# Layer norms from residual rows kept in SBUF, their root on VectorE, and a moved piece of schedule, in a fused attention and feed-forward block

## The chip, the cores and the metric

The kernel runs on one core of one Trainium2 chip. The metric is the device time of one execution in microseconds. The shown runs of the kernel before took 876.0, 876.1 and 879.46 us, so the median is 876.1 us.

## What is computed

One transformer block over 2048 rows of width 512, with a modulation computed from a vector c. The attention has 32 heads of width 16 and works on four segments of 512 rows, with a causal softmax inside a segment and a memory that is carried from one segment to the next. The reference, cut to what matters:

```python
mod = silu(c) @ w_mod                     # six vectors sa, ca, ga, sb, cb, gb
h = layernorm(x) * (1 + ca) + sa
x = x + ga * attention(h)                 # per head: softmax part and memory part, then @ wo
h = layernorm(x) * (1 + cb) + sb
x = x + gb * (((h @ w_gate) * (h @ w_up)) @ w_down)
...
def layernorm(x):  return (x - mean(x)) / sqrt(var(x) + 1e-5)
```

## The kernel before

All products keep float32 accuracy by splitting both factors into a high and a low part and adding three products (names that end in H and L). A segment is four tiles of 128 rows by 512 columns, numbered t = 0 to 3.

**The attention loop** (L1122) has one iteration for each unit v of four heads of a segment, and five slots in an iteration. In a slot TensorE computes scores q (`q_step`, L270), which VectorE reduces to a maximum nm (L291); scores k (`k_step`, L311), which ScalarE exponentiates to pt (L329) and GpSimd masks (selection, L332); and once per iteration the product tb of pt with the values (`av_step`, L336). Between them `fill` (L1053) hands out the rest of the work in pieces from two generators, `fill_a` (L960) and, behind it, `fill_b` (L1023): the next segment's projections, the modulation, the memory, and at the end the output product and the norm ahead of the feed-forward part. A piece counts against a credit, so the written order of the pieces decides which work stands between which scores. `weave(a, b, at)` (L677) puts pieces of b behind chosen pieces of a. In the loop VectorE's instructions are chained in written order (`Chain`, L32, set at L1119); `pin` (L80) keeps an instruction behind the last TensorE instruction in the order of the program without a wait.

**The norms.** `ln_rows` (L167) takes the statistics of four tiles on VectorE (L174, L177), then the root: ScalarE's logarithm and exponential (L181, L183) give y, and one Newton step refines it. That step is five small instructions on 128x4 numbers, L187 to L191, on GpSimd for all norms but segment 0's first, which has them on VectorE. Then VectorE scales the four tiles in place (L194). Norms named a (tiles x) come ahead of attention, norms named c ahead of the feed-forward part. `ln_col` (L202) transposes the scaled tiles on TensorE (ctp), and ScalarE writes chf, the high part chH and GpSimd the low part chL (L222, L223).

**The output product.** `wo_load` (L467) loads a segment's attention rows (orl), `wo_op` (L475) splits them on ScalarE (oH, L497) and VectorE (L480). `wo_mm` (L537) makes one output row tile after the other: four groups of products into wops, then `wo_add` (L533) adds the residual tile xr, which was loaded from x by `xr_load` (L517), and stores the result to x1d in DRAM. For segments 0 and 1 `lnC` (L544) loads the four tiles back from x1d into tiles x (L548) and norms them. Segments 2 and 3 are normed later, in the feed-forward part (L1362 to L1367).

**Order at the end of attention.** `fill_a` ends with the first two output tiles of segment 0 (L1000), since the buffers of its pool are closed ahead of `fill_b` (`open_b`, L955). `fill_b` then makes the last two of segment 0, with the split of segment 1 woven in, all of segment 1 with segment 0's norm, the rest of that norm with segment 2's split, and segment 2 with segment 1's norm and the preparation of the first feed-forward weights (`prep`, L426: loads w, combinations L448, splits AH on ScalarE and AL).

**Modulation.** `mod_acc` (L624) scales four tiles wm on ScalarE (L626) and adds them on GpSimd (L628); `a_mod` (L917) then sums over partitions on TensorE (mc, gbps). Its four pieces for odd outputs are woven into projections K and Q of group 1 (L987 to L989).

Of the kernel before, what the change touches and what calls it, by code (L numbers as in the profile page):

```python
# [18 lines left out]
P = 128  # L19
# [39 lines left out]
def tile_kernel(ctx, tc, x, wq, wk_, wv, wo, beta, w_gate, w_up, w_down, c, w_mod, out):  # L59
# [107 lines left out]
    def ln_rows(pool, xt, s, pfx):  # L167
# [23 lines left out]
        eng.tensor_mul(y, y, b)  # L191
        yield 0.0
# [14 lines left out]
    def ln(pool, hpool, xt, s, sc, sh, pfx, hb, fast, kept_h=None):  # L207
# [5 lines left out]
        for d in range(KT):  # L213
# [15 lines left out]
            if pfx == "c" and d % 2 == 1:  # L229
                yield False  # L230
# [286 lines left out]
    def xr_load(s, pb, ts=range(4), tag="xr"):  # L517
        xrs = []
        for t in ts:
            xr = pb.tile([P, D], F32, tag=tag, name=f"xr{s}_{t}", bufs=2 if pb is wpool else 4)  # L520
            pin(nc.sync.dma_start(xr, x[rows(s, t), :]))
            xrs.append(xr)
        return xrs
# [13 lines left out]
    def wo_mm(s, us, xrs, ts=range(4)):  # L537

        for t, xr in zip(ts, xrs):
            ps = bank(f"wops{s}_{t}")  # L540
            yield from wo_row(ps, t, us, range(NG))
            wo_add(s, t, xr, ps)

    def lnC(s, pool, hpool, xpool, tag, nb):  # L544
        xt = []
        for t in range(4):
            a = xpool.tile([P, D], F32, tag=tag, name=f"x1_{s}_{t}", bufs=nb)
            nc.sync.dma_start(a, x1d[s][t])  # L548
            xt.append(a)
        yield 0.1  # L550
# [4 lines left out]
        for d in (0, 2, 1, 3):  # L555
# [3 lines left out]
            if d > 1:  # L559
                yield False  # L560
# [116 lines left out]
    def weave(a, b, at):  # L677

        i = 0
        for w in a:  # L680
            yield w
            if w:
                for _ in range(at.count(i)):
                    w = next(b, None)
                    if w or w is False:
                        yield w
# [245 lines left out]
    us = [[], [], []]  # L932

# [26 lines left out]
    def fill_a():  # L960
# [5 lines left out]
        for s in range(NSEG):  # L966
# [4 lines left out]
            for g in range(2 if s == 0 else 0, NG):  # L971
# [15 lines left out]
                if g == 1 and 0 < s < 3:  # L987
                    acc = mod_acc(r)
                    K, Q = weave(K, acc, (0, 2)), weave(Q, acc, (0, 2))  # L989
                if s == NSEG - 1 and g == 1:  # L990
                    xr0 = xr_load(0, wpool, (0, 1), "wor")
# [3 lines left out]
                if s == NSEG - 1 and g == NG - 1:  # L995
                    yield from weave(Q, ready, (0, 1, 2, 3))
# [3 lines left out]
                    yield from wo_mm(0, us[0], xr0, (0, 1))  # L1000
# [18 lines left out]
        while memq or memt:  # L1019
            yield mem_step() or 0.0  # L1020
            yield False
# [100 lines left out]
    for v in range(-2, NQ + 1):  # L1122
        rate[0] = 5.8 if v < 20 else 5.2
        on, prev = 0 <= v < NQ, 0 <= v - 1 < NQ
        for slot in range(5):
# [10 lines left out]
            if v == NQ and slot == 0:  # L1136
                assert B["orl_free"]
                o3 = wo_load(3, B["pb"])
                xr3 = xr_load(3, B["pb"])
            if v == NQ and slot == 2:  # L1140
# [379 lines left out]
```

## Time and profile before

| What | Value |
|---|---|
| Median of the shown runs | 876.1 us |
| The profiled execution's own time | 873.19 us |
| Its span | 871.1 us |
| Instructions | 14342 |
| Granted TensorE clock over the span | 0.995 |
| Moved by DMA | 139.45 MB, mean 160 GB/s |

The rows of this trace are of one execution. "L40" is the helper that chains instructions on an engine, so VectorE's rows in the loop are told apart by their tiles. In a row of the timeline come start, duration, engine, line, operation, output and inputs, form and count; a bracket at its end is the idle time of that engine before the row, and what ended it. A row that stands for several instructions of one kind has their count behind x. "PE" is TensorE, "DVE" VectorE, "ACT" ScalarE, "POOL" GpSimd and "SP" the queue that issues most transfers.

### The profile page before, as it was taken

Reading aid. Unit: us, or ns where it says so; the run is one execution under the profiler, and the core shown is the slowest. Engines: PE = TensorE matmul, PEld = TensorE weight load, DVE = VectorE, ACT = ScalarE, POOL = GpSimd, SP = SyncE. Lnnn points to the kernel's source line nnn. Section 1 sums busy time; section 2 is a strip of 40 time slices with the busy share of each in tenths; the row PEclk is TensorE's granted clock in tenths of the full one; section 3 lists DMA queues with packets and bytes.
Section 4 is the critical chain, followed back from the end, with each engine's and each line's share of the span. In section 5 each row is a group of like instructions: output and inputs, shape, how many; then the busy total and the mean of one; then the engine's idle time right before and its main releaser. Section 6 shows DMA issues by size and latency. Waiting matters only on the chain.

```text
span 871.1 us, 14342 instructions
## 1 busy us (share of the span) xinstructions
PE 828.9 (95%) x4823; PEld 581.2 (67%) x4824; DVE 658.9 (76%) x1728; ACT 474.5 (54%) x740; POOL 423.3 (49%) x564
## 2 busy tenths in 40 slices
PE   8989998989999899999988899999999999999998
PEld 5756565656565566655654577888778888887886
DVE  8688776988779877789888769888685966767532
ACT  3758757687676876678544664433354423333321
POOL 4536536565455764487323835998101755650000
PEclk9999999999999999999999999999999999999999
DMA  7773755567647565776794552654305232112032
GB/s 242 227 233 120 226 149 168 187 209 232 194 147 250 188 205 168 250 235 215 235 310 134 170 173 97 181 159 135 109 30 163 77 115 55 50 55 94 0 119 97
DMA packets 111355, 139.45 MB, mean 160 GB/s; under 512 B 18800, under 2 KB 70000, under 8 KB 111280
## 3 DMA queue, kind: packets, MB, share of 16 engines
q1 hardware_dynamic: 106016, 130.91, 48.7%
q10 hardware_dynamic: 5264, 7.62, 2.4%
q8 instruction: 38, 0.62, 0.3%
q14 instruction: 37, 0.30, 0.1%
HBM read 87.48 MB, written 50.76 MB: 159 GB/s over the span
## 4 chain that ended last, share of the span: by engine, by line
PE 66%; DVE 13%; ACT 7%; DMA 5%; POOL 3%; issue 3%; SPq 0%; ACTq 0%; POOLq 0%; DVEq 0%
PE g L90 23%; PE acc L90 14%; PE tb L90 5%; PE k L90 5%; PE q L90 5%; DVE q L40 4%; PE vps L90 4%; PE kps L90 2%; ACT pt L329 2%; PE wops L90 2%; PE qps L90 2%; DVE x L40 2%; DMA x1d<-xr 1%; DMA x<-in_x_dram 1%; PE mz L90 1%
## 5 line engine op out<-in xcount | busy, mean ns | idle before, releaser
L40 DVE CUSTOM_DVE_ANT_0 q<-q,cmask 128x384 f32<-128x384 f32 (+3 forms) x512 | 246.6, 508 | 57.7 <-PE q L90 47.8
L329 ACT ACTIVATE pt<-k 128x1024 f32<-128x1024 f32 x160 | 163.9, 1024 | 74.2 <-PE k L90 57.3
L332 POOL TENSOR_SCALAR_AFFINE_SELECT pt<-pt 128x256 f32<-128x256 f32 (+1 forms) x224 | 105.2, 484 | 154.9 <-ACT pt L329 149.8
L90 PE MATMUL q<-kst,qst 96*128 96x384 bf16 (+3 forms) x512 | 101.6, 300 | 12.1 <-DVE nm L40 11.5
L90 PE MATMUL k<-qst,kst 98*128 98x384 bf16 (+3 forms) x512 | 97.5, 303 | 9.4 <-ACT pt L329 9.1
L448 POOL TENSOR_TENSOR w<-w 128x256 f32<-128x256 f32 (+1 forms) x84 | 73.9, 893 | 56.0 <-DVE t L1205 37.9
L443 POOL TENSOR_TENSOR AL<-w,AH 128x512 fp32r<-128x512 f32 (+1 forms) x42 | 56.4, 1345 | 48.4 <-ACT AH L439 48.3
L90 PE MATMUL tb<-pt,v 128*32 128x512 f32 (+3 forms) x1024 | 77.4, 443 | 1.4 <-POOL pt L332 1.4
L90 PEld LDWEIGHTS <-kst 98*128 98x128 bf16 x512 | 38.5, 99 | 54.3 <-issue 48.0
L40 DVE DVE_READ_ACCUMULATOR2_ANT nm<- 128x1 f32 x512 | 72.3, 141 | 0.0
L90 PEld LDWEIGHTS <-qst 96*128 96x128 bf16 x512 | 43.4, 98 | 39.9 <-issue 15.9
L439 ACT ACTIVATE AH<-w 128x512 fp32r<-128x512 f32 (+3 forms) x88 | 47.2, 565 | 40.0 <-POOL w L448 26.7
L1462 DVE TENSOR_TENSOR mL<-mid,mH 128x512 fp32r<-128x512 f32 (+1 forms) x44 | 32.8, 750 | 41.5 <-ACT mH L1461 41.5
L90 PE MATMUL acc<-DH,mL 128*128 128x512 f32 x144 | 56.6, 393 | 0.9 <-DVE mL L1462 0.9
L90 PE MATMUL acc<-DH,mH 128*128 128x512 f32 x144 | 57.2, 397 | 0.0
L90 PEld LDWEIGHTS tb<-pt,v 128*32 128x32 f32 x1024 | 29.2, 111 | 41.1 <-issue 36.1
L90 PE MATMUL acc<-DL,mH 128*128 128x512 f32 x144 | 56.6, 393 | 0.0
L1461 ACT ACTIVATE mH<-mid 128x512 fp32r<-128x512 f32 (+1 forms) x44 | 27.1, 627 | 52.7 <-PE acc L90 51.5
L1254 ACT ACTIVATE p<-g 128x512 f32<-128x512 f32 (+1 forms) x22 | 13.1, 597 | 75.9 <-PE g L90 75.8
L443 DVE TENSOR_TENSOR AL<-w,AH 128x512 fp32r<-128x512 f32 (+3 forms) x44 | 35.2, 803 | 9.2 <-ACT AH L439 9.0
L358 ACT ACTIVATE tsb<-tb 128x512 f32<-128x512 f32 x32 | 19.1, 598 | 34.0 <-PE tb L90 34.0
L90 PE MATMUL g<-chH,AH 128*128 128x512 f32 (+1 forms) x88 | 34.8, 396 | 0.7 <-ACT p L1254 0.7
(286 smaller groups left out, 2064.3 us busy)
## 6 DMA issues: line engine op xcount, KB each, us to landing
kst<-kd SPq DMA_DIRECT2D x32, 384.0 KB
qst<-qd SPq DMA_DIRECT2D x32, 384.0 KB
td<-tsb ACTq DMA_DIRECT2D x28, 256.0 KB
wm<-in_w_mod_dram SPq DMA_DIRECT2D x24, 256.0 KB
kd<-k SPq DMA_DIRECT2D x16, 384.0 KB
qd<-q SPq DMA_DIRECT2D x16, 384.0 KB
w<-in_w_gate_dram SPq DMA_DIRECT2D x20, 256.0 KB
w<-in_w_up_dram SPq DMA_DIRECT2D x40, 128.0 KB
```

The source lines that it names most:

```text
L40: i = getattr(self.eng, name)(*a, **k)
L90: return pe(nc.tensor.matmul(*a, **k))
L329: lpt[0] = act.activation(pt, kp, AF.Exp, scale=0.25)
L332: sels[u, i] = nc.gpsimd.affine_select(w, w, pattern=[[0, w.shape[1]], [1, P]], compare_op=ALU.is_ge, fill=0.0, base=0, channel_multiplier=-1)
L358: act.activation(tsbs[u], tbs.pop(u), AF.Copy)
L439: i = act.activation(hi[sl], w[sl], AF.Copy)
L443: i = eng.tensor_sub(lo[sl], w[sl], hi[sl].bitcast(F32))
L448: i = ce.tensor_tensor(w[:, o, :, 0:n], w[:, x, :, 0:n], w[:, y, :, 0:n], op=op)
L1254: lcp[0] = act.activation(r["p1"], ps, AF.Copy)
L1461: pin(act.activation(mH[0:n], md[0:n], AF.Copy))
L1462: vec.tensor_sub(mL[0:n], md[0:n], mH[0:n].bitcast(F32))
```

## The change

1. **Residual rows stay in SBUF.** `lnC` for segments 0 and 1 takes the tiles xr that `wo_add` has just written, takes their statistics as they come, and scales them in place. The eight loads from x1d at L548 are gone; the stores to x1d stay, since the end of the kernel reads them (L1485).
2. **Root on VectorE.** The Newton step has four instructions in place of five (the addition of EPS and the multiplication are one) and runs on VectorE for all norms, behind the piece boundary that follows ScalarE's two.
3. **One output tile ahead of the new pool.** `fill_a` makes only tile 0 of segment 0; tiles 1 to 3 follow in `fill_b`. The residual tiles of segment 0 are loaded two groups later.
4. **Places in the weaves.** The norm of segment 1's rows starts a piece later, the modulation pieces of odd outputs stand at K 1, 2, 3 and Q 0 in place of K 0, 2 and Q 0, 2, and `fill_b` weaves norms, splits and the weights' preparation at other places. The fill work is drained at slot 0 of the last iteration, ahead of segment 3's loads.

```diff
@@ ln_rows
-        eng = CV if first else nc.gpsimd
-        eng.tensor_mul(a, y, y)
-        eng.tensor_scalar(b, mv[:, :, 1], 1.0, EPS, op0=ALU.mult, op1=ALU.add)
-        eng.tensor_mul(b, b, a)
-        eng.tensor_scalar(b, b, -0.5, 1.5, op0=ALU.mult, op1=ALU.add)
-        eng.tensor_mul(y, y, b)
-        yield 0.0
+        if not first:
+            yield 0.0
+        for i in (V.tensor_mul(a, y, y), V.scalar_tensor_tensor(b, mv[:, :, 1], EPS, a, op0=ALU.add, op1=ALU.mult),
+                  V.tensor_scalar(b, b, -0.5, 1.5, op0=ALU.mult, op1=ALU.add), V.tensor_mul(y, y, b)):
+            if not first:
+                pin(i)
+        if first:
+            yield 0.0
@@ lnC
-    def lnC(s, pool, hpool, xpool, tag, nb):
-        xt = []
-        for t in range(4):
-            a = xpool.tile([P, D], F32, tag=tag, name=f"x1_{s}_{t}", bufs=nb)
-            nc.sync.dma_start(a, x1d[s][t])
-            xt.append(a)
-        yield 0.1
+    def lnC(s, pool, hpool, xt):
@@ fill_a
-                        K = weave(K, lns, (2, 3) if s > 0 else (3,))
-                        Q = weave(Q, lns, (0, 1, 2) if s > 0 else (0, 1, 2, 3))
+                        K = weave(K, lns, (2, 3) if s > 0 else ())
+                        Q = weave(Q, lns, (0, 1, 2) if s > 0 else (0, 1, 2, 2, 3))
...
-                    K, Q = weave(K, acc, (0, 2)), weave(Q, acc, (0, 2))
+                    K, Q = weave(K, acc, (1, 2, 3)), weave(Q, acc, (0,))
...
-                    yield from wo_mm(0, us[0], xr0, (0, 1))
+                    yield from wo_mm(0, us[0], xr0, (0,))
@@ fill_b
-        rest = wo_mm(0, us[0], xr_load(0, pb, (2, 3)), (2, 3))
+        xr0.extend(xr_load(0, pb, (2, 3), "xr", 4))
         o1 = wo_load(1, pb)
+        lg, op = kept_as("nxt", lnC(0, pb, bc, xr0)), wo_op(1, pb, o1, us[1])
+        yield from weave(wo_mm(0, us[0], xr0, (1, 2, 3)), op, (5, 6, 7, 8, 9), lg, (3, 6, 10))
+        B["o0"] = True
+        xr1 = xr_load(1, pb, range(4), "x1", 4)
         pr = prep(0, "0_0", bc, 1, pb, 1)
-        op = wo_op(1, pb, o1, us[1])
-        yield from weave(rest, op, (4, 5, 6, 7))
-        next(pr)
-        B["o0"] = True
-        lg = lnC(0, pb, bc, pb, "x1", 4)
-        yield from weave(wo_mm(1, us[1], xr_load(1, pb)), chain(op, islice(lg, 10)),
-                         (0, 1, 4, 5, 6, 7, 8, 11, 12, 13, 14))
+        lh, op = kept_as("hf", lnC(1, pb, bc, xr1)), third(pb)
+        yield from weave(wo_mm(1, us[1], xr1), lg, (1, 2, 6, 7, 8, 9, 11, 12, 14, 15),
+                         pr, (3, 13), lh, (5, 9, 13), op, (10, 11, 12, 13, 14))
+        yield from lg
         while "o2" not in B:
             yield None
-        yield from weave(kept_as("nxt", lg), wo_op(2, pb, B["o2"], us[2]), (0, 1, 2, 3, 3))
-        B["orl_free"] = True
-        lg = lnC(1, pb, bc, pb, "x1", 4)
-        rest = weave(wo_mm(2, us[2], xr_load(2, pb)), lg, (0, 3, 4, 5, 6, 7, 10, 11, 12, 13))
-        yield from weave(rest, pr, (1, 8, 9, 14))
-        B["hf"] = yield from lg
+        yield from op
+        xr2 = xr_load(2, pb, range(4), "xr", 4)
+        yield from weave(wo_mm(2, us[2], xr2), lh, (1, 2, 6, 7, 8, 9, 11, 12, 14, 15), pr, (0, 4, 10))
+        yield from lh
```

What moves on the engines, at three places. First, VectorE in the first norm that runs inside the loop (segment 1, ahead of its projections). Each score reduction is a row q and a row nm; x are the segment's tiles, ast and amv the statistics. Before:

```order
L40 BN_STATS ast_0_776<-x_0_690 128x6
L40 BN_AGGR amv_775<-ast_0_776 128x2
L40 ISA q_2_0_796,nm_738<-q_2_0_796,cmask 128x512
L40 ISA nm_738 128x1
L40 ISA q_2_1_799,nm_738<-q_2_1_799,cmask 128x512
L40 ISA nm_738 128x1
L40 BN_STATS ast_1_802<-x_1_692 128x6
L40 BN_AGGR amv_775<-ast_1_802 128x2
L40 BN_STATS ast_2_808<-x_2_694 128x6
L40 BN_AGGR amv_775<-ast_2_808 128x2
L40 ISA q_3_0_814,nm_738<-q_3_0_814,cmask 128x384
```

And in the change, the same place:

```order
L40 ISA q_2_0_791,nm_737<-q_2_0_791,cmask 128x512
L40 ISA nm_737 128x1
L40 ISA q_2_1_794,nm_737<-q_2_1_794,cmask 128x512
L40 ISA nm_737 128x1
L40 BN_STATS ast_0_798<-x_0_689 128x6
L40 BN_AGGR amv_797<-ast_0_798 128x2
L40 BN_STATS ast_1_804<-x_1_691 128x6
L40 BN_AGGR amv_797<-ast_1_804 128x2
L40 ISA q_3_0_810,nm_737<-q_3_0_810,cmask 128x384
```

Tile 0's statistics moved behind two reductions, and tile 2's behind the four of q_3 and one phi (phk, a min and an addition on 128x512) that follow the last row.

Second, GpSimd in the modulation of segment 1's group 1 (wm the modulation tiles, pt selections, kr and k_1_1 the split of the projection K). Before:

```order
L783 TENSOR_TENSOR kr_1_1766<-kf_1_1763,k_1_1_1765 128x512
L332 AFFINE_SELECT pt_3_1819<-pt_3_1819 128x2x128 x2
L628 TENSOR_TENSOR wm_0_1675<-wm_0_1675,wm_2_1679 128x512
L792 TENSOR_TENSOR k_1_1_1765<-kr_1_1766,k_1_1_1765 128x512
L628 TENSOR_TENSOR wm_0_1675<-wm_0_1675,wm_3_1681 128x512
L332 AFFINE_SELECT pt_4_1843<-pt_4_1843 128x4x128
```

And in the change:

```order
L619 TENSOR_TENSOR wm_0_1673<-wm_0_1673,wm_2_1677 128x512
L331 AFFINE_SELECT pt_2_1772<-pt_2_1772 128x2x128 x2
L775 TENSOR_TENSOR kr_1_1764<-kf_1_1761,k_1_1_1763 128x512
L619 TENSOR_TENSOR wm_0_1673<-wm_0_1673,wm_3_1679 128x512
L331 AFFINE_SELECT pt_3_1819<-pt_3_1819 128x2x128 x2
L784 TENSOR_TENSOR k_1_1_1763<-kr_1_1764,k_1_1_1763 128x512
L331 AFFINE_SELECT pt_4_1843<-pt_4_1843 128x4x128
```

The last sum moved ahead of one selection and of the second half of K's split. On ScalarE the scaling of wm_3 moved ahead of the pt of slot 3.

Third, VectorE in segment 0's norm at the end of attention (x_0_1 is tile 1 loaded back from x1d, xr_0 a residual tile, cst and cmv statistics, cy the root, nt part of the scores). Before, statistics of loaded tiles:

```order
L40 BN_STATS cst_1_5969<-x_0_1_5864 128x6
L40 BN_AGGR cmv_5902<-cst_1_5969 128x2
L40 BN_STATS cst_2_5975<-x_0_2_5866 128x6
L40 BN_AGGR cmv_5902<-cst_2_5975 128x2
L40 COPY nt_5992<-ntp_5990 32x128
L40 ISA q_1_0_5995,nm_5962<-q_1_0_5995,cmask 128x384
```

And in the change, at the same place of the same iteration:

```order
L40 BN_STATS cst_0_5973<-xr_0_5825 128x6
L40 BN_AGGR cmv_5972<-cst_0_5973 128x2
L40 TENSOR_TENSOR cya_5874<-cy_5872 128x4
L40 SCALAR_TENSOR_TENSOR cyb_5875<-cmv_5630,cya_5874 128x4
L40 TENSOR_SCALAR cyb_5875<-cyb_5875 128x4
L40 TENSOR_TENSOR cy_5872<-cy_5872,cyb_5875 128x4
L40 TENSOR_SCALAR xr_0_5152<-xr_0_5152,cmv_5630,cy_5872 128x512
L40 COPY nt_5998<-ntp_5996 32x128
```

Segment 0's statistics have moved up, each behind its own residual sum; here its root is refined and its first tile scaled, while the first statistics are of segment 1. Between the sum of segment 0's last residual tile and its scaling stand 18 score reductions. SP's list loses the eight loads, and the loads of segment 1's attention rows (orl) come ahead of the rd, orow and rb transfers and of the store of tile 1, behind which they stood before.

More of the change, by code (lines that the diff above doesn't have):

```diff
@@ L515, in paced, with xr_load @@
             yield False
-    def xr_load(s, pb, ts=range(4), tag="xr"):
+    def xr_load(s, pool, ts, tag, n):
         xrs = []
         for t in ts:
-            xr = pb.tile([P, D], F32, tag=tag, name=f"xr{s}_{t}", bufs=2 if pb is wpool else 4)
+            xr = pool.tile([P, D], F32, tag=tag, name=f"xr{s}_{t}", bufs=n)
             pin(nc.sync.dma_start(xr, x[rows(s, t), :]))
@@ L682, in weave @@
             if w:
[L683 to L686, printed above, removed]
+                for b, at in zip(bs[::2], bs[1::2]):
+                    for _ in range(at.count(i)):
+                        w = next(b, None)
+                        if w or w is False:
+                            yield w
                 i += 1
@@ L932, in tile_kernel @@
     us = [[], [], []]
+    xr0 = []
     def wo_weights():
@@ L1136, in tile_kernel @@
             if v == NQ and slot == 0:
[L1137 to L1140, printed above, removed]
-                btag[:] = ["ms", "lq0", "ms", "lq1"]
                 for f in (fa, fb):
@@ L1144, in tile_kernel @@
                         pass
+                o3 = wo_load(3, B["pb"])
+                xr3 = xr_load(3, B["pb"], range(4), "x1", 4)
+            if v == NQ and slot == 2:
+                btag[:] = ["ms", "lq0", "ms", "lq1"]
                 us3 = []
```

17 lines of the change are left out of this document (8 added, 9 removed).

## The prediction

> **What bounds the kernel now.** I read the page's busy shares first, then the windows by stage, then the rows of the stages that wait.
>
> ```profile
> PE 828.9 (95%) x4823; PEld 581.2 (67%) x4824; DVE 658.9 (76%) x1728; ACT 474.5 (54%) x740; POOL 423.3 (49%) x564
> core 0: us, PE busy (x) PEld busy (x) DVE busy (x) ACT busy (x) POOL busy (x), PEclk, DMA share, GB/s
> 430.00:440.00 10.00, 8.29 (x51) 5.28 (x53) 7.51 (x27) 3.91 (x5) 4.35 (x7) 1.00 0.94 313
> 440.00:460.00 20.00, 19.43 (x143) 11.00 (x143) 18.25 (x63) 9.55 (x12) 4.24 (x9) 1.00 0.97 298
> 460.00:485.00 25.00, 19.37 (x137) 11.81 (x139) 21.12 (x73) 15.32 (x22) 11.90 (x21) 1.00 0.39 128
> 485.00:510.00 25.00, 23.59 (x179) 14.43 (x171) 15.45 (x36) 15.60 (x23) 18.37 (x29) 1.00 0.56 171
> 545.00:871.00 326.00, 320.90 (x1406) 258.53 (x1404) 220.18 (x314) 115.58 (x210) 130.00 (x131) 1.00 0.31 96
> 806.24 60.55 PE acc L90 x264
> ```
>
> TensorE is busy 828.9 of 871.1 us, so 42 us is all that any reordering can win. From 545 on it idles 5.1 us, and 4.3 of these lie behind its last product (806.24 + 60.55 = 866.8). The feed-forward part is full; what the change does there is worth nothing. The change must win in attention, above all from 430 to 510, where TensorE idles 80 - 70.7 = 9.3 us. VectorE is there almost as full (21.1 of 25 us), so both can be the limit.
>
> The stalls of TensorE that the change touches, from its timeline (the bracket is the idle time before the row and what ended it):
>
> ```profile
> 60.09 0.38 PE L90 MATMUL q<-kst,qst 96*128 96x256 bf16 x2 [1.59 <-DVE nm L40]
> 61.00 0.59 PE L90 MATMUL q<-kst,qst 96*128 96x256 bf16 x2 [0.53 <-DVE nm L40]
> 144.12 1.05 PE L90 MATMUL mc<-ones,wm 128*128 128x1 f32 x8 [2.43 <-POOL wm L628]
> 438.99 0.59 PE L90 MATMUL k<-qst,kst 98*128 98x512 bf16 x2 [1.66 <-ACT pt L329]
> 462.78 0.60 PE L90 MATMUL k<-qst,kst 98*128 98x384 bf16 x4 [1.57 <-ACT pt L329]
> 466.08 0.38 PE L90 MATMUL q<-kst,qst 96*128 96x384 bf16 x2 [0.41 <-DVE nm L40]
> 466.73 0.38 PE L90 MATMUL q<-kst,qst 96*128 96x384 bf16 x2 [0.27 <-DVE nm L40]
> 477.16 0.33 PE L93 MATMUL ctp<-ident,x 128*128 128x128 f32 x1 [1.29 <-DVE x L40]
> 477.75 0.66 PE L93 MATMUL ctp<-ident,x 128*128 128x128 f32 x4 [0.27 <-DVE xr L40]
> 480.97 0.60 PE L90 MATMUL k<-qst,kst 98*128 98x256 bf16 x4 [1.25 <-ACT pt L329]
> 483.44 0.59 PE L90 MATMUL k<-qst,kst 98*128 98x512 bf16 x2 [0.55 <-ACT pt L329]
> 500.21 0.64 PE L90 MATMUL tb<-pt,v 128*32 128x256 f32 x8 [1.41 <-POOL pt L332]
> ```
>
> The last nine are 8.7 of the 9.3 us. I take the change in four parts.
>
> **Part 1, statistics of segment 1's rows one slot later.**
>
> ```profile
> 58.22 0.69 DVE L40 BATCH_NORM_STATS2 ast<-x 128x6 f32<-128x512 f32 x1 [1.68 <-DMA x<-in_x_dram]
> L40 DVE CUSTOM_DVE_ANT_0 q<-q,cmask 128x384 f32<-128x384 f32 (+3 forms) x512 | 246.6, 508 | 57.7 <-PE q L90 47.8
> ```
>
> VectorE stands 1.68 us at the third row of x, with the score reductions queued behind it, and TensorE pays 1.59 + 0.53 = 2.1. In the changed order four more reductions (4 x 0.508 = 2.0 us, the mean in the second row) and a phi stand ahead of that row, so it has landed. The fourth row's statistics are next late. I take **-1.5 us**; bounds -2.1 and 0.
>
> **Part 2, modulation sums sooner.**
>
> ```profile
> 141.24 1.16 POOL L792 TENSOR_TENSOR k<-kr,k 128x512 bf16<-128x512 f32 x1
> 142.35 1.72 POOL L628 TENSOR_TENSOR wm<-wm,wm 128x512 f32<-128x512 f32 x1
> 138.18 1.02 ACT L329 ACTIVATE pt<-k 128x1024 f32<-128x1024 f32 x1
> 139.09 0.73 ACT L626 ACTIVATE wm<-wm,s_c 128x512 f32<-128x512 f32 x1
> ```
>
> The last sum ends at 144.07, and TensorE has nothing else from 141.7. In the changed order it stands ahead of L792, and ScalarE scales its row ahead of the pt at 138.18: 138.2 + 0.7 + 1.7 = 140.6, before TensorE arrives. The selection behind it slips by about 1 us, but TensorE needs that only in the next iteration. I take **-2.4 us**; bounds -2.4 and 0. The later sum (gbb) has no stall before it and gives nothing.
>
> **Part 3, the root on VectorE.** Seven norms drop five GpSimd instructions and gain four on VectorE. Before shows these on VectorE once, in segment 0's norm, five of them from the first row to the third:
>
> ```profile
> 9.99 0.17 DVE L40 TENSOR_TENSOR aya<-ay 128x4 f32<-128x4 f32 x1 [0.36 <-ACT ay L40]
> 10.70 0.16 DVE L40 TENSOR_TENSOR ay<-ay,ayb 128x4 f32<-128x4 f32 x1
> 10.89 1.92 DVE L40 TENSOR_SCALAR x<-x,amv,ay 128x512 f32<-128x512 f32 x4
> 174.89 3.94 DVE L40 TENSOR_SCALAR x<-x,amv,ay 128x512 f32<-128x512 f32 x4
> ```
>
> Five take 0.90 us, so four take 0.7 (the fused one isn't shown at this size; its neighbours take 0.16 to 0.19). Two norms lie in the feed-forward part, where VectorE is busy 220 of 326 us: free. Three lie in attention ahead of scalings like that at 174.89, with score reductions queued behind. 3 x 0.7 = 2.1 at most; GpSimd's five hid between selections. ScalarE's root ends well ahead, so no new wait on it. I take two thirds, **+1.4 us**; bounds 0 and 5.7 (each also held up 1.2, next).
>
> ```profile
> 161.37 1.16 POOL L792 TENSOR_TENSOR k<-kr,k 128x512 bf16<-128x512 f32 x1 [0.37 <-ACT k L791]
> 161.64 1.43 DVE L40 SCALAR_TENSOR_TENSOR phk<-phk,rlk 128x512 f32<-128x512 f32 x1
> 60.81 0.69 DVE L40 SCALAR_TENSOR_TENSOR phk<-phk,rlk 128x512 f32<-128x512 f32 x1
> ```
>
> The same VectorE instruction takes 0.69 us alone and 1.43 when it starts inside a GpSimd tensor_tensor; it ends 0.54 after that one. A refinement can so lose up to 1.2 us once. The Trainium skill, page "SBUF — State Buffer", section "Who interferes with whom", says that a VectorE instruction with two SBUF inputs and a GpSimd instruction reading SBUF exclude each other, the later one blocking fully. By that rule the trace agrees, and it speaks against this move: the sum would be +5.7 in this part where every refinement meets such an instruction, +1.4 where none does.
>
> **Part 4, norms of the first two segments from the rows in SBUF.** It removes eight 256 KB reloads and their SP issues, starts the statistics from each row as it is made, and spreads the 16 transposes of segment 0 through TensorE's other work. Five causes make the 8.7 us:
>
> ```profile
> 463.87 0.69 DVE L40 BATCH_NORM_STATS2 cst<-x 128x6 f32<-128x512 f32 x1 [1.93 <-DMA x<-x1d]
> 461.71 1.02 ACT L329 ACTIVATE pt<-k 128x1024 f32<-128x1024 f32 x1 [3.80 <-DMA kst<-kd]
> 437.40 0.63 ACT L497 ACTIVATE oH<-orl 128x512 fp32r<-128x512 f32 x1 [2.59 <-DMA orl<-od]
> 503.43 1.00 DVE L40 TENSOR_SCALAR x<-x,cmv,cy 128x512 f32<-128x512 f32 x2 [5.63 <-POOL cy L191]
> 438.30 5.43 DMA x1d<-xr
> 455.70 8.14 DMA x<-x1d
> ```
>
> - The reload's wait on VectorE (1.93) and the scaling that comes late for the transposes: 0.41 + 0.27 + 1.29 + 0.27 = 2.2, all gone.
> - ScalarE 3.80 us behind a late kst load, while DMA is 94 to 97% busy: 1.57. Four reloads (1 MB, 3.4 us at 298 GB/s) leave this window; I take 1.2.
> - ScalarE 2.59 us at a load of segment 1's attention rows: 1.66. In the changed order these loads stand ahead of a store that held up SP, but their conversion stands a slot sooner too, and the rd, orow and rb loads now queue behind them; I take 0.8.
> - Transposes, conversions and pt crowd ScalarE: 1.25 + 0.55; spread out, 1.2 goes.
> - GpSimd late for the selection: 1.41. Its five root steps leave, its weight work moves up; 0.5.
>
> That is 5.9. Against it: two refinements, 1.4 us of VectorE, half on the path, 0.7; and GpSimd, which now has segment 0's four low parts and the first weights' work at once, may be late for one selection, 1.2. Net **-4.0 us**; bounds -8.7 and +3. The wait of 5.63 at 503.43 goes too, but TensorE had products then.
>
> New wait: scaling in place must wait until the store of the same row has left. Store 5.43 us; in the changed order 18 score reductions stand between the last row's sum and its scaling, 18 x 0.508 = 9.1 us. Covered; uncovered it would hold VectorE up to 5.4 us, with reductions queued behind it. The moved first residual loads and segment 3's loads behind the drained fill work: priced at nothing, covered by TensorE's products at their places; at most +1.
>
> **Sum.** -1.5 - 2.4 + 1.4 - 4.0 = -6.5 against the profiled execution's 873.2 us (span 871.1 and 2.1 around it): 866.7. The median of the runs shown, 876.1, lies 2.9 above the profiled one, so the forecast is **869.6 us**, its own range 867 to 871.6.
>
> **Rivals**, on the median's scale.
> - A, everything goes: -2.1 - 2.4 + 0.7 - 8.7 = -12.5, **863.6**. For: each stall has a cause that the change touches. Against: VectorE at 21.1 of 25 us, so the next wait is near.
> - B, part 4 returns nothing, as GpSimd's crowd or the loads queued behind the early ones cost what the reloads cost: -1.5 - 2.4 + 1.4 = -2.5, **873.6**. For: DMA stays 94% busy at 430 to 460.
> - C, slower: VectorE is the limit and meets GpSimd at every refinement. Five in attention, each 0.7 + 1.2, are +9.5; part 4 returns nothing; -1.5 - 2.4 remain: +5.6, **881.7**. It decides once part 4 returns less than 5.6. Against: only some VectorE rows of before are stretched.
> - D, the change does not do what it says: the in-place scaling waits for its store as long as the reload did. Then part 4's first 2.2 us stay: 871.8; the 18 reductions speak against it.
>
> **How the numbers follow.** Forecast 0.49, A 0.13, B 0.21, C 0.11, D 0.06. A measurement of this kernel tells about 0.5% (4.4 us) from no change. The forecast and A are faster by more (0.62), B and D within (0.27), C slower (0.11). The range reaches from A's time to just over 876: 863.5 to 876.5; it leaves out C and the tails of A and B.
>
> **What would show it.** Right: no wait before mc at 142; no VectorE wait on a DMA at 58 and 463; no x<-x1d reload; 430 to 510 with under 5.5 us of TensorE idle. Wrong: cya or ayb rows of over 0.5 us with q waits behind them; tb waiting for pt selections longer than 1.4 us; xr scalings waiting for x1d stores; a wait on rb.

## The result, and the profile after

The changed kernel is **slower**: 883.6 us in the median of 18 runs (877.5 to 886.9) against 876.0 of the kernel before beside it (18 runs), a ratio of 1.0077 with a 95% interval of 1.0058 to 1.0096. The forecast was 869.6. The profiled execution took 877.5 us, with a span of 875.7 and a granted clock of 0.993; it is the fastest of the 18, and most of the others ran at a clock near 0.985. The clock turns out to be a large part of the loss.

The page's busy shares and the windows, in the stages that the prediction used (columns as there: length, busy time and count on PE, PEld, DVE, ACT and POOL, granted clock, share and GB/s of DMA):

```profile
PE 831.0 (95%) x4824; PEld 581.4 (66%) x4824; DVE 662.3 (76%) x1755; ACT 475.1 (54%) x740; POOL 415.5 (47%) x529
```

```profile
430.00:440.00 10.00, 8.70 (x64) 5.56 (x55) 6.52 (x24) 5.69 (x8) 1.94 (x5) 1.00 0.90 297
440.00:460.00 20.00, 17.71 (x112) 9.51 (x114) 18.19 (x63) 8.18 (x11) 5.41 (x10) 0.91 0.70 214
460.00:485.00 25.00, 21.90 (x162) 12.97 (x151) 23.58 (x78) 16.51 (x23) 12.21 (x18) 1.00 0.52 157
485.00:510.00 25.00, 24.24 (x172) 14.90 (x173) 17.35 (x46) 15.05 (x20) 15.20 (x23) 1.00 0.39 137
```

From 430 to 510 TensorE idles 80 - 72.55 = 7.4 us, where before had 9.3. So idle time did go down, but as many products (510) are busy 1.9 us longer: the clock column has 0.91 at 440 to 460, where before had 1.00.

TensorE's timeline after, at the places that the prediction named and at those where the brackets grew:

```profile
62.56 0.38 PE L90 MATMUL q<-kst,qst 96*128 96x512 bf16 x1 [1.39 <-DVE nm L40]
63.47 0.38 PE L90 MATMUL q<-kst,qst 96*128 96x512 bf16 x1 [0.53 <-DVE nm L40]
...
142.01 0.95 PE L90 MATMUL mc<-ones,wm 128*128 128x1 f32 x8
...
177.70 0.57 PE L90 MATMUL q<-kst,qst 96*128 96x512 bf16 x1 [3.12 <-DVE nm L40]
...
291.41 0.38 PE L90 MATMUL q<-kst,qst 96*128 96x256 bf16 x2 [2.32 <-DVE nm L40]
...
443.45 0.38 PE L90 MATMUL q<-kst,qst 96*128 96x256 bf16 x2 [1.39 <-DVE nm L40]
```

The wait before mc is gone. Grown are the brackets at 177.70 (3.12 us) and 291.41 (2.32): the norms of segments 2 and 3. The same two places in the kernel before:

```profile
179.82 0.38 PE L90 MATMUL q<-kst,qst 96*128 96x512 bf16 x1 [1.38 <-DVE nm L40]
...
289.16 0.38 PE L90 MATMUL q<-kst,qst 96*128 96x256 bf16 x2 [0.53 <-DVE nm L40]
```

At segment 1's norm VectorE no longer waits for the third row. But it now takes the statistics of the third and fourth rows back to back, from 59.91 to 61.6, with the score reductions behind them, and TensorE still idles 1.39 + 0.53 us:

```profile
59.91 0.68 DVE L40 BATCH_NORM_STATS2 ast<-x 128x6 f32<-128x512 f32 x1
...
60.72 0.66 DVE L40 BATCH_NORM_STATS2 ast<-x 128x6 f32<-128x512 f32 x1
```

What VectorE does ahead of 177.70 after, with the four instructions of the refinement and the scalings behind them, and later its wait on rb; then what GpSimd does at that moment:

```profile
171.04 0.16 DVE L40 TENSOR_TENSOR aya<-ay 128x4 f32<-128x4 f32 x1
171.24 1.08 DVE L40 SCALAR_TENSOR_TENSOR ayb<-amv,aya 128x4 f32<-128x4 f32 x1
172.35 0.17 DVE L40 TENSOR_SCALAR ayb<-ayb 128x4 f32<-128x4 f32 x1
172.55 0.40 DVE L40 TENSOR_TENSOR ay<-ay,ayb 128x4 f32<-128x4 f32 x1
172.99 3.73 DVE L40 TENSOR_SCALAR x<-x,amv,ay 128x512 f32<-128x512 f32 x4
...
440.38 0.69 DVE L40 TENSOR_TENSOR orow<-orow,rb 128x512 f32<-128x512 f32 x1 [2.60 <-DMA rb<-rdd]
```

```profile
171.13 1.16 POOL L784 TENSOR_TENSOR q<-qr,q 128x512 bf16<-128x512 f32 x1
```

The fused instruction starts 0.11 us after GpSimd's and ends 0.03 us after it: 1.08 us instead of the 0.16 of its neighbour. The four rows take 1.8 us in place of 0.7, and TensorE's bracket grew by 3.12 - 1.38 = 1.74. That is the mechanism of rival C, near its full price of 1.9.

The windows of one microsecond around that bracket show what follows it:

```profile
176.00:177.00 1.00, 0.00 (x0) 0.00 (x0) 1.00 (x3) 0.14 (x1) 0.99 (x2) 1.00 1.00 331
177.00:178.00 1.00, 0.30 (x1) 0.10 (x1) 0.96 (x6) 0.00 (x0) 0.00 (x0) 0.88 0.82 293
178.00:179.00 1.00, 0.66 (x3) 0.29 (x2) 0.97 (x4) 0.00 (x0) 0.00 (x0) 0.50 0.80 291
179.00:180.00 1.00, 1.00 (x4) 0.81 (x3) 0.96 (x6) 0.63 (x1) 0.00 (x0) 0.50 0.42 151
180.00:181.00 1.00, 1.00 (x7) 0.80 (x5) 0.71 (x4) 0.00 (x0) 0.00 (x0) 0.50 0.23 84
```

The clock is 0.50 for 3.4 us behind the stall (in the next window it is 0.92, then 1.00). Summed, 1 - clock over these windows is 1.70 us: work that TensorE had to do at half speed. The prediction had no such term at all.

Where the time went, by the start of each unit (the first tb row of the unit in the timeline), changed minus before in the two profiled executions:

| Unit | 4 | 5 | 6 | 9 | 15 | 25 | 26 | 29 | 31 |
|---|---|---|---|---|---|---|---|---|---|
| us | -0.5 | -2.2 | -3.8 | +0.8 | +3.2 | +2.4 | +4.9 | +4.9 | +4.0 |

Up to unit 6 the change is ahead (part 2; 1.7 us of it is the half clock that stood behind 144.12 before). The stretch with segment 2's norm costs 4.6 by unit 9, that with segment 3's 2.3 at unit 15, and the end of attention 2.5 at unit 26. The two profiled executions lie 4.3 us apart and the medians 7.6, so this pair shows less of the loss than the timed runs.

### The profile page after: what moved, and what is told of

Read it like the earlier page. It is cut to its first block, busy times and chain, and to the rows that moved or that the text cites. A ratio compares the mean times of both kernels' runs of the same rounds, so it can differ in the third digit from the quotient of the medians.

```text
span 875.7 us, 14338 instructions
## 1 busy us (share of the span) xinstructions
PE 831.0 (95%) x4824; PEld 581.4 (66%) x4824; DVE 662.3 (76%) x1755; ACT 475.1 (54%) x740; POOL 415.5 (47%) x529
## 5 line engine op out<-in xcount | busy, mean ns | idle before, releaser
L447 POOL TENSOR_TENSOR w<-w 128x256 f32<-128x256 f32 (+1 forms) x84 | 71.3, 861 | 58.3 <-DVE t L1200 37.8
L442 POOL TENSOR_TENSOR AL<-w,AH 128x512 fp32r<-128x512 f32 (+1 forms) x42 | 59.3, 1414 | 49.3 <-ACT AH L438 49.2
L1249 ACT ACTIVATE p<-g 128x512 f32<-128x512 f32 (+1 forms) x22 | 13.1, 597 | 78.5 <-PE g L90 78.5
L442 DVE TENSOR_TENSOR AL<-w,AH 128x512 fp32r<-128x512 f32 (+3 forms) x44 | 33.0, 752 | 12.7 <-ACT AH L438 11.9
L90 PE MATMUL g<-t_0H,AH 128*128 128x512 f32 (+1 forms) x88 | 35.1, 399 | 1.7 <-DVE u L1258 1.2
```

The source lines that it names most:

```text
L90: return pe(nc.tensor.matmul(*a, **k))
L442: i = eng.tensor_sub(lo[sl], w[sl], hi[sl].bitcast(F32))
L447: i = ce.tensor_tensor(w[:, o, :, 0:n], w[:, x, :, 0:n], w[:, y, :, 0:n], op=op)
L1249: lcp[0] = act.activation(r["p1"], ps, AF.Copy)
```

## The experiments

For every kernel two numbers are worked out from its timed runs beside the median: **clock loss**, the mean of span x (1 - granted clock), and **rest**, the mean of the time less that loss. The five sets of runs of the kernel before that stood beside these kernels (11 to 29 runs each) have a clock loss of 7.6 to 8.4 and a rest of 868.9 to 869.5 us, so differences of the rest under about 1 us mean nothing here. Of the kernels below, only_root, root_a, root_early, root_a23, rows_sp, only_mod and rows_early have five or six runs and dose has four, and for these it is rather 2 and 3 us. The clock loss counts every stretch at a lower clock, also those at 14 to 19 us, ahead of attention, which 14 of the 19 profiled kernels have, and those behind TensorE's last product.

| Kernel | Median us | Ratio to before, 95% interval | Clock loss | Rest |
|---|---|---|---|---|
| before (beside the first four) | 876.3 | | 7.6 | 869.0 |
| changed | 883.6 | 1.0077 [1.0058, 1.0096] | 12.2 | 870.8 |
| no_root | 874.4 | 0.9983 [0.9962, 1.0004] | 8.7 | 866.0 |
| only_root | 890.4 | 1.0148 [1.0119, 1.0177] | 13.6 | 875.8 |
| only_weaves | 870.1 | 0.9943 [0.9919, 0.9967] | 5.4 | 865.9 |
| only_rows | 878.5 | 1.0013 [0.9990, 1.0035] | 9.3 | 868.7 |
| root_a | 887.0 | 1.0113 [1.0085, 1.0141] | 13.4 | 874.1 |
| root_early | 884.2 | 1.0076 [1.0057, 1.0096] | 13.9 | 870.4 |
| rows_sp | 871.4 | 0.9938 [0.9915, 0.9961] | 5.5 | 866.7 |
| only_mod | 870.7 | 0.9933 [0.9908, 0.9957] | 4.5 | 866.7 |
| dose | 886.4 | 1.0102 [1.0062, 1.0141] | 13.1 | 873.3 |
| first4 | 875.7 | 0.9986 [0.9964, 1.0009] | 7.1 | 869.0 |
| after_sp | 881.7 | 1.0053 [1.0029, 1.0077] | 11.6 | 870.0 |
| root_a1 | 878.7 | 1.0004 [0.9977, 1.0032] | 8.7 | 869.4 |
| root_a23 | 886.3 | 1.0092 [1.0064, 1.0121] | 13.1 | 873.5 |
| early_a23 | 877.2 | 1.0000 [0.9980, 1.0021] | 10.1 | 867.6 |
| root_c | 880.2 | 1.0028 [1.0005, 1.0051] | 8.2 | 872.2 |
| weaves_early | 874.4 | 0.9962 [0.9942, 0.9983] | 8.8 | 865.5 |
| rows_early | 872.2 | 0.9940 [0.9919, 0.9961] | 7.1 | 864.7 |

One run of after_sp, of 2399.77 us, is left out of its last two columns.

### Which part loses

**no_root**: the changed kernel with the five refinement instructions of before (`eng = CV if first else nc.gpsimd`, and the piece boundary behind them).

> The changed kernel with the root's refinement back on GpSimd (part 3 undone, the rest kept). Theory R (the refinement on VectorE, held up behind GpSimd's tensor_tensor with score reductions behind it, makes the loss, partly by half-clock stretches after the longer stalls): R prices the root at 6 to 10 us, so this kernel takes 873 to 878 us, below the changed kernel's 883.6, and its trace has no TensorE stall over 2.4 us at segment 2's norm. Theory S (the loss is part 4's: loads of segment 1's attention rows ahead of rd, orow and rb): this kernel stays at 882 to 885. Theory W (the moved weaves make it): also 882 to 885.

**only_root**: before with the new refinement.

> The kernel before with the root's refinement on VectorE alone (part 3 alone). Theory R: 882 to 886 us, with scalar_tensor_tensor rows of ayb over 1 us and q waits of 2 us and more behind them. Theories S and W: 876 to 878.5 us (seven times four instructions, 0.9 us for each norm at most, most of it beside other work).

**only_weaves**: before with parts 1 and 2.

```diff
-  K = weave(K, lns, (2, 3) if s > 0 else (3,))
-  Q = weave(Q, lns, (0, 1, 2) if s > 0 else (0, 1, 2, 3))
+  K = weave(K, lns, (2, 3) if s > 0 else ())
+  Q = weave(Q, lns, (0, 1, 2) if s > 0 else (0, 1, 2, 2, 3))
-  K, Q = weave(K, acc, (0, 2)), weave(Q, acc, (0, 2))
+  K, Q = weave(K, acc, (1, 2, 3)), weave(Q, acc, (0,))
```

> The kernel before with parts 1 and 2 alone (statistics of segment 1's rows a piece later, modulation sums sooner). All theories but W: 872 to 874.5 us, by the 3.8 us that the changed kernel is ahead at the start of unit 6. Theory W: 877 us or more, with half-clock stretches at other places.

**only_rows**: the changed kernel with parts 1, 2 and 3 undone.

> The kernel before with part 4 alone (norms of the first two outputs from rows in SBUF, one output tile ahead of the new pool, the weaves at the end of attention). Theory S: 880 to 884 us, with a wait of VectorE on rb and a half-clock stretch at about 445. Theory R: 874 to 878 us, as the reloads' waits go and the wait on rb takes their place.

Measured: 874.4, 890.4, 870.1 and 878.5 us. Theory R stands: the root costs 883.6 - 874.4 = 9.2 us in the changed kernel (8.3 by the means of the runs) and 14.1 on the kernel before. Theory W falls, the weaves gain 6.2. Theory S is too strong, but part 4 gains nothing either: +2.2 alone, where the interval includes no change, and +4.3 on top of the weaves.

### Where the root is paid

**root_a**: the new refinement only `if pfx == "a"`.

> The kernel before with the refinement on VectorE in the norms ahead of attention only; the norms ahead of the feed-forward part keep it on GpSimd. In the kernel with part 3 alone (890.4 us) the profiled run lost 10.6 us by the start of unit 9 and 13.6 by unit 16, and 3 more behind unit 27. If the price is paid where score reductions stand behind the refinement (theory R): 885 to 889 us. If it is paid at the end of attention, in the two norms of the first outputs: 876 to 880 us.

**root_early**: only_root with the boundary where it was.

```diff
-        if not first:
-            yield 0.0
         for i in (V.tensor_mul(a, y, y), ...):
             ...
-        if first:
-            yield 0.0
+        yield 0.0
```

> Part 3 alone again, but with the refinement one piece earlier: directly behind the last tile's statistics, and not directly ahead of the scalings. The same instructions, on the same engine. Theory R1 (the price is the place: behind a GpSimd tensor_tensor and ahead of four scalings, so that the score reductions come late): 877 to 882 us, scalar_tensor_tensor rows of ayb at about 0.2 us, no TensorE stall over 2.5 us at segment 2's norm. Theory R2 (four more instructions on VectorE cost the same wherever they stand, and VectorE now waits for ScalarE's root in order): 886 to 891 us.

root_a took 887.0 us, most of the 14. root_early took 884.2 at a clock of 0.984, between the two expectations: its rest fell from 875.8 to 870.4, near before's, as R1 has it, but its clock loss stayed. So five more kernels take one group of norms at a time, by a condition on (pfx, s). First, segment 0's norm alone (first4):

> The kernel before with nothing changed but segment 0's first norm, whose refinement, on VectorE in both kernels, takes four instructions in place of five. The kernels with the root on VectorE all lose 12 to 14 us to the granted clock, also where the refinement stands early and its stalls at segments 2 and 3 are gone. If the start of the kernel is the cause: 880 to 884 us at a clock of 0.985. If the stalls in attention are: 875 to 878 us at 0.991.

875.7 us: not the start. Then segment 1's (root_a1):

> The kernel before with the refinement on VectorE in segment 1's norm alone (the first that stands among score reductions). In the profiled runs its place shows TensorE stalls of 1.6 us with the refinement on GpSimd and 2.2 to 2.4 with it on VectorE, then 6.8 us of half clock in place of 3.4. If that place carries the clock's loss that stays when the refinement is moved earlier: 879 to 882 us. If it carries no more than the 0.7 us of instructions: 875.5 to 877.5 us.

878.7 us, with a ratio of 1.0004: next to nothing. Then those of segments 2 and 3, late as in the change (root_a23) and a piece earlier (early_a23), and those ahead of the feed-forward part (root_c):

> The kernel before with the refinement on VectorE in the norms of segments 2 and 3 alone. Theory R (late, behind a GpSimd tensor_tensor, ahead of scalings that are held up too; TensorE stalls of 3.12 and 2.3 us in place of 1.4 and 0.5, each with half clock behind it): 6 to 9 us, 882 to 885 us. If segment 1's norm makes the loss: 876 to 878.5 us.

> The same two norms with the refinement one piece earlier. Theory R: the loss goes, 875 to 878 us, clock at 0.990 to 0.993. If VectorE's instructions cost the same wherever they stand: as the run with them late.

> The kernel before with the refinement on VectorE in the four norms ahead of the feed-forward part alone. By the difference of the runs with all norms and with the first kind alone (890.4 and 887.0, against 876.3 and 877.6 of before): 880 to 882 us. If the two kinds don't add up: 876 to 878 us.

root_a23 took 886.3 us, early_a23 877.2, root_c 880.2. **The two norms of segments 2 and 3, refined late, carry most of the price**, 9.9 us by the medians and 8.1 by the ratio; a piece earlier the same eight instructions cost nothing that can be measured (ratio 1.0000; the rest is 1.9 lower than before's and the clock loss 2.4 higher). By their medians root_a1 adds 2.2 and root_c 3.7 (0.4 and 2.5 by the ratios).

A piece earlier is not free everywhere. root_early, which has all norms a piece earlier, lies 7.0 above early_a23, and its trace shows a new stall at segment 1's norm:

```profile
65.71 0.36 DVE L40 TENSOR_TENSOR aya<-ay 128x4 f32<-128x4 f32 x1 [1.55 <-ACT ay L183]
...
67.65 0.38 PE L90 MATMUL q<-kst,qst 96*128 96x512 bf16 x1 [3.12 <-DVE nm L40]
```

There VectorE comes to the refinement before ScalarE has made y and waits 1.55 us, as theory R2 had feared; TensorE idles 3.12 us, and half clock begins 1.5 us later. Late, in root_a1, the same row has no wait. No run moves segment 1's refinement or the norms ahead of the feed-forward part earlier by themselves, so how the 7.0 us divide is open.

Why a piece earlier helps isn't quite R1's reason. VectorE in root_a23, then in early_a23, and TensorE behind each:

```profile
176.76 1.08 DVE L40 SCALAR_TENSOR_TENSOR ayb<-amv,aya 128x4 f32<-128x4 f32 x1
...
178.51 3.74 DVE L40 TENSOR_SCALAR x<-x,amv,ay 128x512 f32<-128x512 f32 x4
```

```profile
183.22 0.58 PE L90 MATMUL q<-kst,qst 96*128 96x512 bf16 x1 [3.12 <-DMA rb<-rdd]
```

```profile
172.34 0.92 DVE L40 SCALAR_TENSOR_TENSOR ayb<-amv,aya 128x4 f32<-128x4 f32 x1
...
177.03 2.03 DVE L40 TENSOR_SCALAR x<-x,amv,ay 128x512 f32<-128x512 f32 x4
```

```profile
174.76 0.38 PE L90 MATMUL q<-kst,qst 96*128 96x384 bf16 x2 [0.64 <-DVE nm L40]
...
186.16 0.38 PE L90 MATMUL q<-kst,qst 96*128 96x512 bf16 x1 [0.18 <-DVE nm L40]
```

The early refinement is held up too (0.92, where R1 had expected 0.2), but no longer back to back with the four scalings: TensorE pays 0.64 and 0.18 instead of 3.12 (the name of a DMA in that bracket is of the last release by the profile; the engine that works there is VectorE). And the scalings themselves take 2.03 us instead of 3.74 when they start past GpSimd's row. By these rows, a delay of VectorE reaches TensorE only by what exceeds the products already handed out; two delays in one piece exceed it, in two pieces they don't. Part of it is luck of the place, as the scalings of the kernel before (3.94 us, with 1.38 on TensorE) were held up too; no run takes the two effects apart.

### The hold-up and the clock, by themselves

> Computes nothing of the block: 18 bursts of 56 TensorE products with gaps between them that VectorE makes (0 to 5 statistics instructions of 0.69 us, three times each), and then seven kinds of VectorE instruction, each alone and beside a row of nine GpSimd tensor_tensor instructions of 128x512. Theory H (a gap of TensorE brings a stretch of half clock behind it): none behind the gaps under about 1.3 us, one behind nearly every gap over 2.6 us, some between. If the granted clock falls for other reasons: no relation to the gap. Theory L (a VectorE instruction that starts inside a GpSimd tensor_tensor is held up to its end): the kinds with two SBUF inputs go up from about 0.16 us (128x4) and 0.69 us (128x512) by up to 1.2 us for those that meet one, the statistics and the one that reads PSUM don't. The scaling with one SBUF input is open: its rows of 0.85 us on average in attention, against 0.48 in segment 0, say that it is held up too.

The VectorE part, each kind first beside nine GpSimd instructions and then without them, x40, x14 and x12:

```profile
293.97 16.41 DVE L40 SCALAR_TENSOR_TENSOR sn<-sm,so 128x4 f32<-128x4 f32 x40
...
310.41 7.83 DVE L40 SCALAR_TENSOR_TENSOR sn<-sm,so 128x4 f32<-128x4 f32 x40
...
343.05 15.62 DVE L40 TENSOR_SCALAR b<-a,sm,so 128x512 f32<-128x512 f32 x14
...
358.71 8.13 DVE L40 TENSOR_SCALAR b<-a,sm,so 128x512 f32<-128x512 f32 x14
...
392.87 8.70 DVE L40 BATCH_NORM_STATS2 st<-a 128x6 f32<-128x512 f32 x12
...
402.44 8.69 DVE L40 BATCH_NORM_STATS2 st<-a 128x6 f32<-128x512 f32 x12
```

Theory L holds, and the open kind is answered: the fused instruction goes from 7.83 to 16.41 us and the scaling, with one input in SBUF, from 8.13 to 15.62; statistics don't change (nor does a subtraction that reads PSUM, 8.61 and 8.62). The Trainium skill, page "SBUF — State Buffer", section "Who interferes with whom", says this of tensor_scalar as well, which can run in a mode that takes both ports; the prediction quoted only its sentence on two inputs, and so left the four scalings, 128x512 each, out of the account. Whether the scaling runs in that mode here no run shows. In the kernel before the scalings were held up as well (3.94 us for four at 174.89, against 1.92 at 10.89), so its sum for part 3 does not change by them.

The TensorE part, gaps and what stands behind them:

```profile
58.19 0.38 PE L40 MATMUL ps<-go,wu 128*128 128x512 bf16 x1 [2.36 <-DVE go L40]
...
73.52 0.38 PE L40 MATMUL ps<-go,wu 128*128 128x512 bf16 x1 [3.09 <-DVE go L40]
```

```profile
74.00:75.00 1.00, 1.00 (x6) 0.37 (x5) 0.00 (x0) 0.00 (x0) 0.81 0.00 0
75.00:76.00 1.00, 1.00 (x4) 0.45 (x3) 0.00 (x0) 0.00 (x0) 0.50 0.00 0
76.00:77.00 1.00, 1.00 (x4) 0.30 (x2) 0.00 (x0) 0.00 (x0) 0.50 0.00 0
77.00:78.00 1.00, 1.00 (x4) 0.32 (x3) 0.00 (x0) 0.00 (x0) 0.50 0.00 0
```

Gaps of 0.44, 0.91, 1.63 and 2.36 us between bursts of 12 to 15 us leave the clock at 1.00, all twelve; 3.09 and 3.82 are followed by half clock, all six. In the attention of the 19 profiled kernels shorter stalls do it too; whether other idle time close by is the reason was not tried. TensorE's stalls between 24 and 545 us by length, and how many had a fall of the clock beginning in them or within 4 us behind:

| Stall, us | 0.7 to 1.3 | 1.3 to 2.0 | 2.0 to 2.6 | over 2.6 |
|---|---|---|---|---|
| Followed by half clock | 13 of 175 | 18 of 66 | 20 of 30 | 8 of 8 |

All 55 falls in attention begin in or behind a stall of 0.7 us or more, though the stretches from such a stall to 4 us behind it are only 14% of attention, and each is 1.7 or twice 1.7 us of lost clock. So theory H holds with a probability, not with an edge. The Trainium skill, page "TensorE: Matmul & The Clock Gate", section "HAM oscillation — how this bites in real kernels", gives "no PE-idle gaps >~3.4µs" as the rule; the gaps by themselves come near it (3.09 falls, 2.36 doesn't), the kernel doesn't: 2.0 to 2.6 us is enough two times in three.

> Parts 1 and 2 alone (870.1 us) with statistics of a constant tile added on VectorE ahead of score reductions, 2, 4 and 6 of them in units where TensorE has no stall, twice each: 1.4, 2.8 and 4.2 us of VectorE, 16.8 in all. If TensorE's cover is about 1 us, the stalls are about 0.4, 1.8 and 3.2 us, 10.8 together. Theory H (stalls of over 2 us bring half clock, 1.7 us lost each): one episode behind each of the two longest, perhaps behind the middle ones, 884 to 888 us. Rival (the granted clock falls at random or at fixed places): 880 to 882 us, no low clock at these places.

```diff
+            if slot == 1 and v in DOSE:            # {10: 2, 11: 4, 12: 6, 18: 2, 19: 4, 20: 6}
+                for _ in range(DOSE[v]):
+                    st = ap.tile([P, 6], F32, tag="dst", ...)
...
+                    pin(vec.bn_stats(st, hmg.rearrange("p a h e -> p (a h e)")[:, 0:512]))
```

886.4 us: the rest is 7.4 above only_weaves (10.8 had been estimated), the clock loss 7.7 above it. In the profiled execution TensorE's longest stalls there are

```profile
236.92 0.38 PE L90 MATMUL q<-kst,qst 96*128 96x512 bf16 x1 [1.22 <-DVE nm L40]
```

and 1.45 at 355.17, shorter than estimated; two falls of 1.70 follow the first group (at 224 and 238), none the second. Delays of VectorE that have nothing to do with a root cost clock as well. By the four timed runs it is about as much as the stalls themselves, but their clocks reach from 0.980 to 0.992, and the places within one run aren't regular.

### Part 4: what takes the gain back

VectorE's waits on rb in no_root, and SP's issues ahead of the first:

```profile
437.88 0.69 DVE L40 TENSOR_TENSOR orow<-orow,rb 128x512 f32<-128x512 f32 x1 [2.65 <-DMA rb<-rdd]
...
469.42 0.69 DVE L40 TENSOR_TENSOR orow<-orow,rb 128x512 f32<-128x512 f32 x1 [2.42 <-DMA rb<-rdd]
```

```profile
426.29 2.41 SPq L469 DMA_DIRECT2D orl<-od  x4
429.71 0.54 SPq L396 DMA_DIRECT2D rd<-td  x1
431.84 0.52 SPq L397 DMA_DIRECT2D orow<-td  x1
433.37 0.58 SPq L407 DMA_DIRECT2D rb<-rdd  x1
```

Four loads of segment 1's rows stand ahead of rd, orow and rb, and rb is issued 7 us behind the first of them.

**rows_sp** issues them in a piece of their own, and the first weights' loads four pieces later:

```diff
-        o1 = wo_load(1, pb)
-        lg, op = kept_as("nxt", lnC(0, pb, bc, xr0)), wo_op(1, pb, o1, us[1])
-        yield from weave(wo_mm(0, us[0], xr0, (1, 2, 3)), op, (5, 6, 7, 8, 9), lg, (3, 6, 10))
+        lg, op = kept_as("nxt", lnC(0, pb, bc, xr0)), second(pb)        # second: wo_load, a piece, wo_op
+        yield from weave(wo_mm(0, us[0], xr0, (1, 2, 3)), op, (2, 6, 7, 8, 9, 10), lg, (3, 6, 10))
...
-                         pr, (3, 13), lh, ...
+                         pr, (7, 13), lh, ...
```

> Parts 1, 2 and 4 with the root on GpSimd (874.4 us) and one thing moved: the four loads of segment 1's attention rows are issued two pieces later, behind rd, orow and rb, and the first weights' loads four pieces later, behind the next rb. Theory S (part 4 loses through VectorE's two waits on rb, 2.65 and 2.42 us, which TensorE's stalls of 1.56 + 0.53 and 2.41 follow): both waits under 0.6 us and 869.5 to 872 us. Rival (part 4 loses because splits, transposes and scalings crowd into the same units, whatever the transfers do): 873.5 to 876 us, with the stalls ended by other releasers.

871.4 us, in the range of theory S, though only one of the two waits fell under its 0.6. SP and VectorE there:

```profile
422.81 0.54 SPq L396 DMA_DIRECT2D rd<-td  x1
423.40 0.52 SPq L397 DMA_DIRECT2D orow<-td  x1
423.96 0.58 SPq L407 DMA_DIRECT2D rb<-rdd  x1
424.59 5.04 SPq L469 DMA_DIRECT2D orl<-od  x4
```

```profile
462.24 0.69 DVE L40 TENSOR_TENSOR orow<-orow,rb 128x512 f32<-128x512 f32 x1 [0.51 <-DMA rb<-rdd]
```

rb goes out 9.4 us sooner, and the second wait falls from 2.42 to 0.51; at the first VectorE still idles 1.87 us, but the trace names no transfer for it. The gain is in the clock loss (8.7 to 5.5), not in the rest (866.0 and 866.7). Which of the two moved groups of loads brings it was not tried.

> The changed kernel (883.6 us) with the loads of segment 1's attention rows two pieces later and the first weights' four pieces later, as in the kernel with the root on GpSimd, where this gave 3.9 us against the runs of before. If the wait on rb and the root cost apart from each other: 878.5 to 881 us. If the root's stalls alone bound the end of attention: 882.5 to 884.5 us.

881.7 us, between the two expectations: the same mend gives about 2 us where the root is on VectorE, by the ratios 1.0077 - 1.0053, whose intervals overlap.

### Parts 1 and 2 apart, and the mended whole

> Part 2 alone, on the kernel before. Parts 1 and 2 together took 870.1 us. If part 1 gives what the start of unit 0 shows in the profiled run (0.06 us): 869.5 to 871 us. If part 1 gives the 1.5 us predicted of it: 871.3 to 872.5 us.

870.7 us: part 2 alone has all of the gain, part 1 nothing that can be measured.

> Parts 1 and 2 (870.1 us) with the refinement of segments 2 and 3 on VectorE, one piece early, which alone made no difference (ratio 1.0000) but had 1.9 us less at full clock than the runs of before. If the two add: 868 to 870.5 us. If VectorE's early instructions take back what the weaves gave: 872 us or more.

874.4 us, no faster than only_weaves: they don't add.

> All four parts, mended: the refinement of segments 2 and 3 on VectorE one piece early and the other norms' on GpSimd, and the loads of segment 1's attention rows behind rb (871.4 us with the root on GpSimd everywhere). If the idea of the change is sound and only these two faults made the loss: 868 to 872 us, as the forecast of 869.6. If residual rows in SBUF bring new waits: 873 us or more.

872.2 us, with the lowest rest of all, 864.7. only_mod, rows_sp, rows_early and only_weaves (ratios 0.9933 to 0.9943, intervals overlapping) all beat both kernels; the simplest of them is one line.

## Why the prediction was wrong

By the medians of only_weaves, no_root and the changed kernel, parts 1 and 2 together gave -6.2 us (forecast -3.9), part 4 on top of them +4.3 (forecast -4.0), and part 3 on top of these +9.2 (forecast +1.4).

- **Part 1 (-1.5).** Its wait is gone: the third row's statistics at 59.91 have no bracket. But TensorE's stall went from 1.59 + 0.53 to 1.39 + 0.53. The fourth row's statistics aren't late, as the prediction feared; they now stand with the third row's in one block of 1.7 us ahead of the score reductions, which hold TensorE as the wait did. That block was not priced. Measured: nothing (870.1 with part 1 beside part 2, 870.7 without).
- **Part 2 (-2.4).** Right: no wait before mc at 142.01, and the rest of only_mod is 869.2 - 866.7 = 2.5 lower. The chip gave another 3.8 in clock loss (8.3 to 4.5): of the ten profiled kernels that keep the 2.4 us stall ahead of mc, nine have half clock from it on. One fall is 1.7; where the rest of the 3.8 comes from, six runs don't settle.
- **Part 3 (+1.4, bounds 0 and 5.7): the step that failed most.** The place, the hold-up and its size (1.2 once per norm) were all in the prediction, and the sum with every refinement held up, +5.7, was written beside the value taken. "I take two thirds" of the instructions alone had no row behind it: that the refinement would miss GpSimd's instructions at segment 2's norm was hoped, not looked up. Measured 9.2 by the medians and 8.3 by the means: 4.8 of these are rest (870.8 - 866.0), within the bounds, and 3.5 clock, which no bound held. The prediction's own sign of being wrong, ayb rows of over 0.5 us with q waits behind them, is what the trace shows (1.08).
- **Part 4 (-4.0, bounds -8.7 and +3).** The reloads' waits went as said. "The rd, orow and rb loads now queue behind them; I take 0.8" is the step that failed: the queue was seen and entered as a smaller gain, while the wait on rb (2.60 and, in no_root, a second of 2.42) was a new loss, larger than the wait removed on VectorE (1.93). Alone it is +2.2 (interval of the ratio 0.9990 to 1.0035), on the weaves +4.3; mended it gives 871.4 against 870.1 of the weaves alone, so even then its gain isn't seen. What holds TensorE up at 430 to 510 once the old waits are gone (chf, scalings and splits, by the brackets) was not taken apart by a run.
- **The missing term.** A stall of TensorE was priced at its own length. In this kernel it was also followed by 1.7 us or more of lost clock, in 7% of the stalls of about 1 us and in all eight over 2.6. The kernel before loses 7.6 us to the clock in all, the changed one 12.2, only_mod 4.5. The trace of before had it: its mean clock is 0.72 from 60 to 66 us and 0.81 from 143 to 152, behind the stalls at 60.09 and 144.12, and the span's 0.995 was read as nothing.
- **Rivals.** C was right in kind (VectorE the limit, GpSimd in the way, part 4 returning under 5.6) and 1.9 us short; it had 0.11. Two of the five meetings that it counted cost most of it, more than half of the rise is clock (4.6 us against the runs of before), which it had not, and it kept part 1's gain, which did not come: that its number is so near is in part luck. D did not happen: the scalings of xr have no wait on a store.

## What to carry to other kernels

Price a stall of the busiest engine at its length plus what its clock does afterwards, and read the granted clock in windows of a microsecond behind each stall before summing. Before moving small instructions to VectorE, look up in the trace what GpSimd runs at that very place. A piece earlier can cost nothing, as at segments 2 and 3, but only where the input is there by then: at segment 1 VectorE waited 1.55 us for it. When loads move ahead in a queue, the first question is which small transfer with an engine waiting for it now stands behind them.

## What the runs showed of the hardware

- A stall of about 3 us was followed by 3.4 us, at times 6.8, of half TensorE clock (all six gaps over 3 us in micro, all eight stalls over 2.6 in attention). How much clock is lost differs between runs of one program; in the changed kernel time and clock loss correlate at 0.92, from 877.5 us at a clock of 0.993 to 886.9 at 0.982.
- A one-input scaling in fp32 (128x512, 0.58 us alone) is held up by GpSimd's tensor_tensor as two-input instructions are; statistics, and a subtraction with one input in PSUM, are not.
- Both sides pay: beside these scalings GpSimd's nine instructions took 12.46 us, beside two-input VectorE instructions of 128x512 14.60, beside statistics 12.02.
